# A PSUM bank of its own for one product of the last block, and the same steps in a new order

## The chip, the cores and the metric

The kernel runs on one core of one Trainium2 chip. The metric is the device time of one execution in microseconds, as the median of several runs; lower is better. The core's engines are named as in the profile: PE (TensorE, matmuls), PEld (its weight loads), DVE (VectorE), ACT (ScalarE), POOL (GpSimd) and SP (SyncE, which issues nearly all transfers). PSUM, into which TensorE writes, has eight banks here, each a tile `ps` of 128 × 512 float32.

## The reference

An attention with a decaying state is followed by a two-layer network with a leaky ReLU. B, H, S, D are 4, 8, 768 and 48; the network has 3072 tokens, 384 columns and 2048 hidden columns.

```python
for t in range(S):
    cur = np.einsum('bhd,bhe->bhde', u[None] * kt, vt)
    y[:, :, t] = np.einsum('bhd,bhde->bhe', rt, state + cur)
    state = wt[:, :, :, None] * state + np.einsum('bhd,bhe->bhde', kt, vt)
...
x = y.transpose(0, 2, 1, 3).reshape(B * S, H * D)
h = x @ w_in
out = np.maximum(0.01 * h, h) @ w_out
```

Inputs and outputs are float32; the kernel multiplies in bfloat16 and accumulates in float32.

## The kernel before, in words

**Attention.** The tokens are cut into 24 chunks of 128. Each chunk's four inputs w, k, r and v are loaded by SP (line 841; the first two chunks of each batch are loaded together, line 626) into one of ten `in` buffers. ACT takes logarithms of w (L851); TensorE sums them along the chunk with a triangular matrix (L857) and makes the chunk's total decay (L860); DVE subtracts a chunk's own part (L869); ACT takes exponentials (L878, L883, L887); DVE multiplies r and k by them (`rk`, L541). `rk` is then transposed to `rkT`: for some chunks by TensorE (L552) with a copy out of PSUM on DVE or ACT (L557, L559), for 13 others by a transposing DMA on SP's queue (L904). TensorE makes the scores from `rkT` (L998), DVE masks them (`m`, L928), and TensorE makes the output from the old state (L964) and from the scores (L969). POOL computes the bonus of the current token (L571, L575, L583) and casts v (L591); DVE adds the bonus into `y` (L614). The state goes on by L938, L953 and POOL's L915. `y` is transposed into `xT`, by TensorE (L600, copied by L605 or L607) or by a transposing DMA (L983, 8 chunks).

**Network.** The tokens go through it in 15 blocks of one or two chunks. For each block, up-projections (L1160) fill PSUM banks (`hp`, or `hq` in the last three blocks), and ACT applies the leaky ReLU into `g` (L1175). Down-projections (L1190) accumulate 16 hidden slices into a bank `op`; DVE or ACT copies it out (L1201, L1203) and SP stores it (L1207). The weights are loaded by SP (L462, L467) and cast to bfloat16 by POOL, DVE or ACT (L484, L486, L488).

**The last three blocks** use seven half-size products in place of eight (function `seven`). DVE forms differences of weight quarters once (`mix`, L1044) and, for each block, sums of parts of `g` (L1075, into an `in` buffer and into `g` itself). TensorE runs the products (L1092). They land in the halves of three banks:

```python
b1, b2, b3 = Buf("ps", "op"), Buf("ps", "op2"), Buf("ps", "op2")
px, py, pv, pw, pz = (lambda b=b, x=x: b.t[:, x * HN : (x + 1) * HN]
                      for b, x in ((b1, 0), (b1, 1), (b2, 0), (b2, 1), (b3, 0)))
...
s_c22 = plus(ob, hi(ob), lo(eb), pv, [s_e3, s_7], [eb, b2])
s_3 = products(14.5, b2, [(pw, lambda: sv(2), lambda: qs[:, 1, 1])], [*s_sum["s4"], s_7], stop=True)
s_c12 = plus(oa, hi(oa), lo(eb), pw, [s_e3, s_3], [eb, b2])
```

`take` copies a half bank to SBUF (L1106 on DVE, L1108 on ACT), `plus` adds a half bank to such a copy on DVE (L1113). The four results are c11 and c12 (the two halves of the first chunk's rows, in `oa`) and c21 and c22 (the second chunk's, in `ob`). In the last block c11 and c12 are stored as two halves of 96 KB, and `ob` as one piece of 192 KB (L1143). The products have names: s_1 (px, py), s_7 and then s_3 in one bank (pv and pw), s_6 and s_5 (px, accumulated), s_4 (pz).

**The order of the work.** Each piece above is recorded as a step with its engines and lengths, the steps that it waits for, the buffers that it reads or takes, and a priority. A planner (`Plan.order`) then plays the kernel through with these lengths: an engine that comes free takes the ready step of lowest priority number whose buffers are free. What comes out is one fixed order for all engines, and the buffer that each step gets. The table `RANK` adds a number of its own to the priority of every step, and `FORCE` binds some steps to one of the engines that could run them. On the chip each engine, and SP's queue, works off its instructions in that fixed order, and each waits by semaphores for what it needs. Where the plan leaves TensorE idle in the first 24 us, filler matmuls on zeros are put in (L1232).

Of the kernel before, what the change touches and what calls it, by code (L numbers as in the profile page):

```python
# [23 lines left out]
class Plan:  # L24
# [138 lines left out]
RANK = {0: -59.43, 1: -52.42, 2: -98.27, 3: -101.28, 4: -69.43, 5: 951.62, 6: -68.29, 7: -162.82, 8: -162.92,  # L163
# [144 lines left out]
def kernel(  # L308
# [41 lines left out]
    blocks = [2, 1, 1, 1, 1, 2, 2, 2, 2, 2, 1, 1, 2, 2, 2]  # L350
# [53 lines left out]
    with tc.manual_schedule():  # L404
# [644 lines left out]
        def seven(nb, chs, g, g_done):  # L1049
# [4 lines left out]
            qs = quarters(w_out_b)  # L1054
# [4 lines left out]
            def sv(x):  # L1059
                return sm.t[:].bitcast(BF16).rearrange("p (x i n) -> p x i n", x=3, n=L)[:, x]  # L1060

            groups = [range(0, 4), range(4, 8)] if nb == len(blocks) - 1 else [range(0, 8)]
            s_sum = {}
# [36 lines left out]
            lo = lambda b: lambda: b.t[:, 0:HN]  # L1100
# [166 lines left out]
```

## Time and profile before

| | |
|---|---|
| time, median of 3 runs | 181.15 us |
| the three runs | 181.15, 180.34, 185.15 us |
| profiled execution: time | 180.35 us |
| profiled execution: span of its trace | 178.6 us |
| mean granted TensorE clock | 0.997 |
| busy: PE, DVE, ACT, POOL | 171.6, 130.2, 116.1, 104.7 us |
| transfers | 34.43 MB in 116716 packets, of which 109137 under 512 B |

The span runs from the first to the last instruction of the profiled execution, and the time includes what lies around it. A row of the chain or the timeline gives the start in the span, the length, the engine and the line; "x8" is the number of instructions in one row, and a bracket tells how long the engine was idle ahead of it and what ended that. A row of waits has the engine, who waited for whom, the total in us, the number of times and the longest.

### The profile page before, as it was taken

What the parts mean: (1) busy time and instruction counts of PE and PEld (TensorE: products, weight loads), DVE (VectorE), ACT (ScalarE), POOL (GpSimd) and SP (SyncE); (2) the same over time, 40 slices, a digit from 0 to 9 for tenths busy, and PEclk for the clock granted to TensorE, in tenths of its full rate; (3) what the DMA queues carried; (4) which work ended last, traced back from release to release, by engine and by line L of the source; (5) the groups of instructions that cost most, each with busy time, mean ns of one, the idle gap of its engine ahead of it and who ended that gap; (6) DMA issues with size and microseconds to landing.
All of it is one profiled execution on the core that took longest, in us unless ns stands there. A gap on an engine that the chain in (4) does not pass through costs nothing.

```text
span 178.6 us, 5383 instructions
## 1 busy us (share of the span) xinstructions
PE 171.6 (96%) x2110; PEld 135.0 (76%) x2110; DVE 130.2 (73%) x265; ACT 116.1 (65%) x259; POOL 104.7 (59%) x139
## 2 busy tenths in 40 slices
PE   7898999999999999999999999999999999999992
PEld 2556888866878787787688777777688788799991
DVE  7498953368877989769776379699778778786462
ACT  5668967675887679666467974287385587822830
POOL 5989633665985686947619849339773557400000
PEclk9999999999999999999999999999999999999998
DMA  5999999999999998999999999999999985913004
GB/s 138 261 283 313 372 375 368 186 198 173 205 168 225 190 212 143 193 231 150 170 161 195 196 224 242 137 194 207 145 193 173 245 166 129 232 25 114 2 22 156
DMA packets 116716, 34.43 MB, mean 193 GB/s; under 512 B 109137, under 2 KB 115922, under 8 KB 116690
## 3 DMA queue, kind: packets, MB, share of 16 engines
q1 hardware_dynamic: 116688, 34.09, 96.7%
q8 instruction: 16, 0.26, 0.7%
q14 instruction: 10, 0.08, 0.2%
q10 hardware_dynamic: 2, 0.00, 0.0%
HBM read 25.17 MB, written 4.72 MB: 167 GB/s over the span
## 4 chain that ended last, share of the span: by engine, by line
PE 58%; DMA 14%; SPq 11%; DVE 4%; POOL 4%; ACT 4%; issue 3%; POOLq 0%; DVEq 0%
PE ps L1160 23%; PE ps L1190 14%; SPq L841 10%; PE ps L1092 8%; DMA in<-in_k_dram 5%; DMA xT<-y 3%; DMA in<-in_v_dram 3%; DMA rkT<-rk 2%; POOL ru L571 2%; PE ps L998 2%; DMA in<-in_r_dram 2%; PE ps L552 1%; PE ps L969 1%; PE ps L1232 1%; PE ps L964 1%
## 5 line engine op out<-in xcount | busy, mean ns | idle before, releaser
L1160 PE MATMUL ps<-xT,w_in_b 128*128 128x256 bf16 (+1 forms) x720 | 72.2, 251 | 0.4 <-DMA xT<-y 0.3
L1175 ACT ACTIVATE g<-ps 128x512 bf16<-128x512 f32 x96 | 55.9, 595 | 24.5 <-PE ps L1160 21.3
L1160 PEld LDWEIGHTS <-w_in_b 128*128 128x128 bf16 x720 | 57.6, 98 | 8.5 <-issue 0.5
L1190 PE MATMUL ps<-w_out_b,g 128*128 128x384 bf16 x288 | 55.8, 326 | 0.0
L1190 PEld LDWEIGHTS <-g 128*128 128x128 bf16 x288 | 25.9, 98 | 12.4
L541 DVE TENSOR_TENSOR rk<-in,ps 128x384 bf16<-128x384 f32 x48 | 24.8, 549 | 9.6 <-ACT ps L887 2.2
L571 POOL TENSOR_TENSOR ru<-in,ub 128x384 f32<-128x384 f32 x24 | 23.9, 998 | 13.0 <-DMA in<-in_k_dram 10.6
L928 DVE TENSOR_TENSOR m<-ps,maskb 128x512 bf16<-128x512 f32 x40 | 25.3, 682 | 2.8 <-PE ps L998 2.6
L575 POOL TENSOR_TENSOR ru<-ru,in 128x384 f32<-128x384 f32 x24 | 24.5, 1026 | 3.0 <-DMA in<-in_r_dram 2.5
L915 POOL TENSOR_TENSOR sb<-s,a 128x384 bf16<-128x384 f32 x18 | 15.2, 844 | 11.6 <-ACT a L878 11.5
L583 POOL TENSOR_TENSOR vs<-in,dg 128x384 f32<-128x384 f32 x20 | 17.6, 883 | 4.6 <-DVE dg L579 1.7
L591 POOL CAST vb<-in 128x384 bf16<-128x384 f32 x24 | 12.0, 503 | 9.5 <-DMA in<-in_v_dram 8.3
L869 DVE TENSOR_TENSOR ci<-ps,lw 128x384 f32<-128x384 f32 x20 | 11.1, 555 | 8.3 <-PE ps L860 5.1
L579 DVE TENSOR_REDUCE dg<-ru 128x8 f32<-128x384 f32 x24 | 13.0, 547 | 2.0 <-POOL ru L575 2.0
L851 ACT ACTIVATE lw<-in 128x384 bf16<-128x384 f32 x20 | 10.4, 522 | 5.8 <-DMA in<-in_w_dram 5.7
L614 DVE TENSOR_TENSOR y<-ps,vs 128x384 bf16<-128x384 f32 x20 | 11.0, 553 | 3.9 <-PE ps L969 1.9
L878 ACT ACTIVATE a<-ps 64x4 f32<-64x4 f32 x36 | 6.1, 168 | 8.1 <-DVE ci L869 5.7
L1203 ACT COPY o<-ps 128x384 f32<-128x384 f32 x14 | 6.7, 478 | 5.8 <-PE ps L1190 5.8
L1232 PE MATMUL ps<-zeros 128*128 128x128 bf16 (+1 forms) x41 | 9.1, 337 | 1.3 <-DVE zeros L405 1.3
L887 ACT ACTIVATE ps<-ci 128x384 f32<-128x384 f32 x20 | 9.7, 485 | 0.7 <-DVE ci L869 0.7
L883 ACT ACTIVATE ps<-ps 128x384 f32<-128x384 f32 x20 | 9.4, 469 | 0.8 <-DVE ci L869 0.6
L953 DVE TENSOR_TENSOR s<-ps,sb 128x384 f32<-128x384 f32 x14 | 7.7, 552 | 1.7 <-PE ps L938 1.5
(103 smaller groups left out, 220.9 us busy)
## 6 DMA issues: line engine op xcount, KB each, us to landing
out_dram<-o SPq DMA_DIRECT2D x23, 192.0 KB, 3.1
in<-in_w_dram SPq DMA_DIRECT2D x20, 192.0 KB, 4.3
in<-in_k_dram SPq DMA_DIRECT2D x20, 192.0 KB, 4.7
in<-in_r_dram SPq DMA_DIRECT2D x20, 192.0 KB, 4.3
in<-in_v_dram SPq DMA_DIRECT2D x20, 192.0 KB, 4.2
in<-in_moe_w_out_dram SPq DMA_DIRECT2D x4, 768.0 KB, 10.6
in<-in_moe_w_in_dram SPq DMA_DIRECT2D x4, 384.0 KB, 7.1
in<-in_moe_w_in_dram SPq DMA_DIRECT2D x2, 768.0 KB, 8.9
```

The costliest lines, as they stand in the source:

```text
L541: (nc.gpsimd if e == "POOL" else nc.vector).tensor_tensor(out=o, in0=x, in1=i, op=ALU.mult)
L571: lambda e: nc.gpsimd.tensor_tensor(out=ru.t[:], in0=kv(), in1=ubv, op=ALU.mult),
L575: lambda e: nc.gpsimd.tensor_tensor(out=ru.t[:], in0=ru.t[:], in1=rv(), op=ALU.mult),
L579: lambda e: nc.vector.tensor_reduce(out=dg.t[:], in_=ru.t[:], axis=AX.X, op=ALU.add),
L583: lambda e: nc.gpsimd.tensor_tensor(out=vs.t[:], in0=vv(), in1=dg.t[:].unsqueeze(2).to_broadcast([128, H, D]), op=ALU.mult),
L841: nc.sync.dma_start(out=part(i)(), in_=src[b, :, t0 : t0 + L, :].rearrange("h p d -> p h d"))
L915: lambda e: nc.gpsimd.tensor_tensor(out=sb.t[:].rearrange("p g a d -> p (g a) d"), in0=s_in.t[:].rearrange("p g a d -> p (g a) d"), in1=a_ ...
L928: lambda e, par=par: nc.vector.tensor_tensor(out=m.t[:, par, :, :], in0=sc[par].t[:].rearrange("p (g t) -> p g t", g=NP), in1=maskb[:].uns ...
L1092: nc.tensor.matmul(o(), lhsT=x()[:, i, :], rhs=y()[:, i, :], start=fresh, stop=(stop and i == ii[-1]), skip_group_check=True)
L1160: nc.tensor.matmul(hp.t[:, a * N : (a + 1) * N], lhsT=w_in_b[:, t, (j + a) * 128 : (j + a + 1) * 128], rhs=xT[:, t, c0 : c0 + N], start=(a ...
L1175: lambda e, hp=hp, g=g, j=j, J=J, N=N: nc.scalar.activation(out=g.t[:, j : j + J, 0:N], in_=hp.t[:, 0 : J * N].rearrange("p (a n) -> p a n ...
L1190: nc.tensor.matmul(op.t[:, 0:DM], lhsT=g.t[:, j, off : off + 128], rhs=w_out_b[:, j, :], start=(j == 0), stop=(j == NJ - 1))
```

## The change

The edit to the code is in `seven`, for the last block alone: pw gets a bank `b4` of its own (`own`), so the product s_3 starts a bank (`start=own`) and no longer waits for s_7, which wrote pv. Besides, `RANK` has new numbers for 1082 of its 1088 steps, and `FORCE` binds other steps to engines (63 entries against 69). Both tables come from a search for an order, this time with smaller lengthenings of the steps while it searched. The steps themselves and their recorded lengths stay as they were. Lines behind the tables move down by 2 to 6: L1092 of before is L1096 of after, L1113 is L1117, L1143 is L1149, L1160 is L1166, L841 is L843, L904 is L906.

```diff
-RANK = {0: -59.43, 1: -52.42, 2: -98.27, 3: -101.28, 4: -69.43, 5: 951.62, 6: -68.29, 7: -162.82, 8: -162.92,
...
+RANK = {0: -32.93, 1: -33.92, 2: -148.03, 3: -147.74, 4: -75.54, 5: -50.53, 6: -92.91, 7: -193.52, 8: -193.62,
...
-FORCE = {4: "ACT", 24: "DVE", 27: "ACT", 30: "DVE", 33: "ACT", 47: "ACT", 57: "ACT", 59: "ACT", 60: "ACT", 62:
...
+FORCE = {4: "ACT", 6: "DVE", 24: "DVE", 27: "ACT", 33: "DVE", 47: "ACT", 62: "ACT", 80: "ACT", 83: "ACT", 86:
...
             b1, b2, b3 = Buf("ps", "op"), Buf("ps", "op2"), Buf("ps", "op2")
+            own = nb == len(blocks) - 1
+            b4 = Buf("ps", "op3") if own else b2
             px, py, pv, pw, pz = (lambda b=b, x=x: b.t[:, x * HN : (x + 1) * HN]
-                                  for b, x in ((b1, 0), (b1, 1), (b2, 0), (b2, 1), (b3, 0)))
+                                  for b, x in ((b1, 0), (b1, 1), (b2, 0), (b4, 1 - own), (b3, 0)))
...
-            s_3 = products(14.5, b2, [(pw, lambda: sv(2), lambda: qs[:, 1, 1])], [*s_sum["s4"], s_7], stop=True)
-            s_c12 = plus(oa, hi(oa), lo(eb), pw, [s_e3, s_3], [eb, b2])
+            s_3 = products(
+                14.5, b4, [(pw, lambda: sv(2), lambda: qs[:, 1, 1])], [*s_sum["s4"], None if own else s_7], start=own,
+                stop=True)
+            s_c12 = plus(oa, hi(oa), lo(eb), pw, [s_e3, s_3], [eb, b4])
```

More of the change, by code (lines that the diff above doesn't have):

```diff
@@ L162 @@
 TY = (0.95, 24, 0.7, -0.6)
-RANK = {0: -59.43, 1: -52.42, 2: -98.27, 3: -101.28, 4: -69.43, 5: 951.62, 6: -68.29, 7: -162.82, 8: -162.92,
[133 rows of a table removed]
-FORCE = {4: "ACT", 24: "DVE", 27: "ACT", 30: "DVE", 33: "ACT", 47: "ACT", 57: "ACT", 59: "ACT", 60: "ACT", 62:
-    "ACT", 80: "ACT", 83: "DVE", 86: "DVE", 89: "ACT", 103: "DVE", 113: "DVE", 115: "DVE", 116: "ACT", 120:
-    "ACT", 122: "POOL", 124: "POOL", 126: "ACT", 128: "ACT", 129: "POOL", 131: "POOL", 132: "ACT", 134: "DVE",
-    135: "POOL", 137: "DVE", 138: "DVE", 141: "POOL", 143: "DVE", 158: "DVE", 160: "ACT", 187: "ACT", 189:
-    "DVE", 198: "ACT", 202: "DVE", 240: "ACT", 262: "DVE", 278: "ACT", 280: "ACT", 309: "DVE", 311: "ACT",
-    325: "DVE", 384: "DVE", 422: "ACT", 436: "DVE", 493: "DVE", 613: "ACT", 737: "ACT", 771: "ACT", 785:
-    "ACT", 799: "ACT", 849: "ACT", 855: "ACT", 877: "DVE", 883: "ACT", 905: "ACT", 933: "ACT", 939: "DVE",
-    953: "ACT", 967: "ACT", 1003: "ACT", 1031: "DVE", 1034: "ACT", 1039: "ACT", 1076: "ACT", 1081: "ACT"}
+RANK = {0: -32.93, 1: -33.92, 2: -148.03, 3: -147.74, 4: -75.54, 5: -50.53, 6: -92.91, 7: -193.52, 8: -193.62,
[135 rows of a table added]
+FORCE = {4: "ACT", 6: "DVE", 24: "DVE", 27: "ACT", 33: "DVE", 47: "ACT", 62: "ACT", 80: "ACT", 83: "ACT", 86:
+    "DVE", 116: "DVE", 118: "DVE", 124: "DVE", 126: "ACT", 128: "ACT", 129: "DVE", 131: "ACT", 137: "DVE",
+    141: "DVE", 143: "POOL", 144: "ACT", 158: "DVE", 160: "DVE", 173: "ACT", 189: "DVE", 198: "DVE", 238:
+    "DVE", 240: "DVE", 254: "DVE", 311: "ACT", 325: "DVE", 341: "ACT", 343: "DVE", 422: "DVE", 436: "ACT",
+    444: "DVE", 493: "DVE", 501: "DVE", 605: "DVE", 613: "ACT", 737: "ACT", 771: "DVE", 785: "ACT", 799:
+    "ACT", 821: "ACT", 827: "DVE", 849: "ACT", 855: "DVE", 877: "ACT", 883: "ACT", 905: "ACT", 911: "DVE",
+    933: "DVE", 939: "ACT", 953: "ACT", 967: "ACT", 995: "DVE", 998: "DVE", 1003: "ACT", 1031: "DVE", 1034:
+    "ACT", 1039: "ACT", 1076: "ACT"}
 @with_exitstack
```

268 rows, old and new, of the table RANK are left out of this document.

## The prediction

> **What bounds the kernel now.** I read the page's busy shares and the slices first.
>
> ```profile
> span 178.6 us, 5383 instructions
> PE 171.6 (96%) x2110; PEld 135.0 (76%) x2110; DVE 130.2 (73%) x265; ACT 116.1 (65%) x259; POOL 104.7 (59%) x139
> DMA  5999999999999998999999999999999985913004
> q1 hardware_dynamic: 116688, 34.09, 96.7%
> PE 58%; DMA 14%; SPq 11%; DVE 4%; POOL 4%; ACT 4%; issue 3%; POOLq 0%; DVEq 0%
> ```
>
> Two things are full at once. TensorE is busy for 171.6 of 178.6 us, and the transfer engines are busy in nearly every slice (4.5 us each) up to 143 us. The chain of waits shares the span out accordingly: TensorE 58%, transfers and SP's queue 25%. DVE, ACT and POOL have 48, 63 and 74 us of idle time. The table by stage shows when each limit holds:
>
> ```profile
> core 0: us, PE busy (x) PEld busy (x) DVE busy (x) ACT busy (x) POOL busy (x), PEclk, DMA share, GB/s
> 0.00:19.00 19.00, 16.17 (x224) 10.00 (x225) 15.08 (x43) 12.79 (x28) 15.23 (x31) 1.00 1.05 256
> 19.00:64.00 45.00, 44.84 (x601) 35.47 (x601) 30.72 (x59) 33.41 (x72) 29.50 (x37) 1.00 1.04 241
> 128.00:152.00 24.00, 24.00 (x326) 20.02 (x324) 18.51 (x35) 17.33 (x41) 13.87 (x18) 1.00 0.95 184
> 157.00:168.00 11.00, 11.00 (x129) 10.43 (x125) 7.90 (x19) 4.51 (x9) 0.00 (x0) 1.00 0.20 57
> 168.00:176.00 8.00, 7.39 (x86) 6.95 (x83) 4.80 (x14) 2.68 (x7) 0.00 (x0) 1.00 0.19 66
> ```
>
> The transfer share (rows overlap, so it can pass 1) is 0.95 or more in the stages shown up to 152 us and 0.2 after 157 us, where TensorE alone sets the pace. What links the two stages is in the chain in order of time:
>
> ```profile
> 19.05 1.47 PE ps L1160 x12
> ...
> 144.38 0.17 PE ps L964 x4
> ...
> 152.55 3.59 DMA rkT<-rk
> 156.18 0.40 PE ps L998 x8
> 157.05 1.32 PE ps L1092 x16
> 158.55 0.20 PE ps L969 x8
> 163.37 5.24 PE ps L1160 x48
> 168.60 5.32 PE ps L1092 x64
> 174.41 0.37 DVE o L1113
> 174.82 0.83 PE ps L1092 x8
> 175.68 0.36 DVE o L1113
> ```
>
> The up-projections begin at 19.05. The last transposing DMA that carries rkT lands, the last scores (L998) run at 156.18, the last attention products (L969) at 158.55, and from there TensorE has only up-projection matmuls (L1160) and the products of the last blocks (L1092). These stand 5.24/48 = 0.109 and 5.32/64 = 0.083 us apart. The program has 54 of the first kind and 128 of the second behind that last L969 group: 158.75 + 54 × 0.109 + 128 × 0.083 = 175.26. The last group in fact ends at 175.65. So one stall of 0.4 us is in this stage, and the rows at 174.41 and 174.82 show it.
>
> **The change, first part: the bank.** The stall, in the timeline of the end:
>
> ```profile
> 164.06 5.18 ACT L1175 ACTIVATE g<-ps 128x512 bf16<-128x512 f32 x8 [3.64 <-PE ps L1160]
> ...
> 173.42 1.15 PE L1092 MATMUL ps<-in,g 128*128 128x192 bf16 x12
> 174.32 0.10 PEld L1092 LDWEIGHTS <-in 128*128 128x128 bf16 x1
> 174.82 0.82 PE L1092 MATMUL ps<-w_out_b,in 128*128 128x192 bf16 x8 [0.25 <-DVE o L1113]
> 175.68 0.36 DVE L1113 TENSOR_TENSOR o<-ps,o 128x192 f32<-128x192 f32 x1 [0.65 <-PE ps L1092]
> ```
>
> The last product (s_3, into pw) goes into the right half of the bank whose left half (pv) DVE is still adding from. The twelve matmuls before it would let it start at 173.42 + 12 × 0.083 = 174.42; its weights are in at 174.32, but it starts at 174.82, when DVE's add is done. With pw in a bank of its own the order of the changed program has no wait on any of those eight matmuls, so 0.40 us goes. The new bank was an up-projection bank; its reader, ACT's L1175, is through by 169.24, five us earlier, so nothing new is waited for. The last two products also change places: s_3 now runs before s_4, so the last matmul group is s_4, and three adds of 0.36 us follow: c12 can start 0.66 us (8 × 0.083) before the last group ends, c22 is next, c21 waits for that end. DVE then has 0.66 us for two adds of 0.36 us, so c21 is at most 0.1 us late. TensorE ends at 175.65 − 0.40 = 175.25, the last add at about 175.65 instead of 176.04.
>
> The price is in the store behind it. Now the last store is the whole 192 KB row block (c21 and c22) and not the half (c12):
>
> ```profile
> out_dram<-o SPq DMA_DIRECT2D x3, 192.0 KB, 2.0
> out_dram<-o SPq DMA_DIRECT2D x2, 96.0 KB, 1.6
> ```
>
> These are the stores of the end alone. 2.0 − 1.6 = 0.4 us goes back. The bank is worth −0.40 + 0.05 + 0.40 = +0.05 us: nothing. Bounds: −0.4 (the larger store is hidden after all) and +0.4 (c21 late by a whole add).
>
> **The change, second part: the order.** The comparison of the two programs, engine by engine, shows what the new ranks and forced engines do.
>
> SP: the same 144 transfers, of which the first 14 stand in the same order. The last rkT transpose is the 134th in both, and the 133 ahead of it are the same in kind and number (80 loads of single chunks, 17 stores, 12 rkT and 6 xT transposes, 8 paired loads, 10 weight loads). While the transfer engines stay full, its landing is set by that volume and not by its order. Behind it stand the same ten transfers. Cost 0; the stream's fill is the cover, and rival 1 is what happens without it.
>
> PE: the same 2069 working matmuls; the fillers (L1232) go from 15 wide and 26 narrow ones to 17 and 22.
>
> ```profile
> L1232 PE MATMUL ps<-zeros 128*128 128x512 bf16 x15 | 5.8, 514 | 1.3 <-DVE zeros L405 1.3
> L1232 PE MATMUL ps<-zeros 128*128 128x128 bf16 x26 | 4.2, 235 | 0.0
> ```
>
> 2 × 0.51 − 4 × 0.24 = +0.1 us, in a stage where TensorE waits for the first chunks. Behind the last L969 group stand the same 54 and 128 matmuls. Between the last scores and the end stand 66 up matmuls and 136 products instead of 54 and 144, with one attention group fewer: 12 × 0.109 − 8 × 0.083 = +0.64, less 0.37 (eight L969 and four L964 matmuls, 0.20 and 0.17 us): +0.3 us if the last rkT lands at the same moment. Before has waits of its own in this stretch (158.37, the end of sixteen L1092 from 157.05, to 158.55), 0.2 us. I take +0.1, bounds −0.2 and +0.3.
>
> POOL, DVE and ACT: four weight casts leave POOL (7 to 3), two for DVE, two for ACT; copies out of PSUM move both ways. In all DVE has 7 instructions more, ACT 3 and POOL 4 fewer.
>
> ```profile
> L484 POOL CAST w_out_b<-in x3: 827/1214/1215, 27.0 to 33.4; 128x768 bf16<-128x768 f32 x3
> L486 DVE CAST w_out_b<-in x5: 549/559/1200, 25.6 to 33.4; 128x768 bf16<-128x768 f32 x5
> 27.04 1.20 DVE L486 CAST w_out_b<-in 128x768 bf16<-128x768 f32 x1 [0.46 <-DMA in<-in_moe_w_out_dram]
> 31.14 1.22 POOL L484 CAST w_out_b<-in 128x768 bf16<-128x768 f32 x1 [1.27 <-DMA in<-in_moe_w_out_dram]
> ```
>
> DVE gets about 7 × 0.55 = 3.9 us on 130.2, POOL loses 4 × 0.83 = 3.3 us. All of it lies beside TensorE, which is full from 19 to 64 us (44.84 of 45.00). If that cover is gone in one place, the cost is one copy, 0.36 to 0.56 us. I take 0, bounds −0.5 and +0.5.
>
> One rule speaks against moving casts to DVE: the Trainium skill, "SBUF — State Buffer", section "SBUF: two separate sides", says that DVE and GpSimd share a port pair as an exclusive lock, and that whichever starts first holds it for its whole instruction. The trace agrees: at 27.04 the DVE cast, started just after POOL's, took 1.20 instead of 0.56 us, and at 31.14 POOL's, started after DVE's, took 1.22 instead of 0.83. By it two more DVE casts would cost POOL up to 2 × 0.39 = 0.8 us, against the 3.3 us that POOL is relieved of; the sum would stay where it is.
>
> **The sum.** +0.05 (bank) + 0.1 (fillers) + 0.1 (last stretch) + 0 (the rest) = +0.25 us, and its bounds together are −1.0 and +1.3. The profiled execution took 180.35 us for its span of 178.6, so it comes out at 180.6, between 179.4 and 181.7. The three runs before were 180.34, 181.15 and 185.15, so that execution is at their low end and 0.8 under their median. The new median should scatter like them; I put 0.2 on it: 180.8 us.
>
> **Rivals.** 1, slower: the transfer stream runs dry behind a waiting SP. SP issues in order, so a transpose whose source is late holds every load behind it.
>
> ```profile
> SPq L904 <- PE ps L1160: 5.9, 5, 2.1
> SPq L904 <- DVE rk L541: 2.9, 1, 2.9
> in<-in_w_dram SPq DMA_DIRECT2D x20, 192.0 KB, 4.3
> ```
>
> Of the waits that have loads behind them the longest is now 2.9 us, and a load lands 4.3 us after its issue, so what is in flight covers them. It decides where waits in a row exceed 4.3 us. The new order puts two xT and one rkT transpose in a row (107th to 109th). Were each to wait 2.9 us, 8.7 − 4.3 = 4.4 us would be lost in a full stream and never come back: 184.8 us, 2.4% slower. Against it: those three would all have to be as late as the latest one now. Two such waits would cost 1.5 us, 181.9. (The Trainium skill, "DMA: Bandwidth & Descriptors", section "Anatomy of one DMA — SWDGE (gpsimd) path", says that semaphore waits happen on the issuing sequencer before dispatch; this is that rule at work, and SP's waits above agree.)
>
> 2, faster: the new order removes TensorE's other waits. Idle is 178.6 − 171.6 = 7.0 us, of which 2.95 lie after the last matmul (175.65) and 1.3 before the first:
>
> ```profile
> PE ps L1232 <- DVE zeros L405: 1.3, 1, 1.3
> PE ps L1160 <- DMA xT<-y: 0.3, 1, 0.3
> ```
>
> 2.75 us are left in many small pieces. All of them gone would give 177.6, 1.5% faster; over 2% would need an earlier start as well, and the first 14 transfers are unchanged.
>
> 3, the bank does nothing: another wait takes its place, such as the products that wait for ACT's copy of px. Then the larger store alone counts, +0.4 on 180.35 and the other terms' 0.2: 181.0. It lies inside the forecast's bounds and is counted apart for its cause.
>
> **How the numbers follow.** Forecast (179.4 to 181.7) 0.63; rival 1 0.14, half of it over 2%; rival 2 0.13, a third of it over 2% by way of the start; rival 3 0.10. Two per cent, 3.6 us, is about what a measurement of this kernel tells from no change. So faster 0.05; slower 0.07 and 0.02 for scatter like the run of 185.15, 0.09; same 0.86. The range takes half of rival 2 and the two-wait form of rival 1 with the runs' own scatter: 179.0 to 183.0.
>
> **What would show it.** Right: the last L1092 group has no idle time before it, TensorE's last group ends about 19 us after the last rkT landing, the last store is 192 KB with about 2.0 us to landing, and the transfers stay full to 143 us. Wrong: a slice of the transfers below 8 before that, SP waits over 4.3 us, the last scores later than 157 us, or a first up-projection more than 1 us away from 19.05.

## The result, and the profile after

The changed kernel takes 181.15 us (median of 20 runs), before 181.53 us (20 runs, the three listed above among them), and the ratio is 1.0057, 95% interval 1.003 to 1.0084. The ratio compares fast runs alone, and ten of before's runs (181.92 to 186.97 us) lie more than 1.5% above its fastest, which is why it is over 1 although before's median is the higher one. So the changed kernel is slower by about 1.0 us. Two later measurements on two chips, beside before each time, gave 1.0077 (1.0052 to 1.0102) and 1.0091 (1.0064 to 1.0117), that is 1.4 and 1.6 us. I had forecast no change.

The page of the profiled execution, 0.9 us longer than that of before:

```profile
span 179.5 us, 5373 instructions
PE 171.4 (96%) x2104; PEld 134.4 (75%) x2108; DVE 132.9 (74%) x272; ACT 115.4 (64%) x256; POOL 100.3 (56%) x135
DMA  5999999998999999999899999999999996813004
PE 66%; DMA 12%; DVE 6%; POOL 5%; ACT 4%; SPq 3%; issue 2%; DVEq 0%; ACTq 0%; POOLq 0%
```

TensorE has the same work within 0.2 us, and the transfers are as full as before. What changed is the chain: TensorE's share rose from 58 to 66%, SP's queue fell from 11 to 3%. The table by stage, with the columns and the stages of the one before:

```profile
0.00:19.00 19.00, 16.20 (x209) 9.57 (x213) 15.32 (x43) 12.89 (x28) 15.23 (x31) 1.00 1.05 257
19.00:64.00 45.00, 43.84 (x595) 34.07 (x595) 32.60 (x65) 31.64 (x68) 25.02 (x33) 1.00 1.16 237
128.00:152.00 24.00, 23.46 (x321) 19.60 (x321) 18.26 (x35) 16.47 (x39) 16.18 (x21) 1.00 1.00 190
168.00:176.00 8.00, 7.93 (x93) 7.59 (x90) 5.39 (x16) 3.29 (x8) 0.00 (x0) 1.00 0.15 53
```

From 19 to 64 us TensorE is busy for 43.84 us where it was 44.84, from 128 to 152 us for 23.46 where it was 24.00; from 64 to 128 us it waits 0.39 us less. So TensorE now waits in two stages in which it had hardly waited. The first of these two rows of waits (who waited for whom, total, times, longest) has no counterpart in before; for the second, before had 0.4 us:

```profile
PE ps L859 <- ACT lw L853: 0.8, 2, 0.4
PE ps L554 <- DVE rk L543: 0.6, 2, 0.5
```

L859 is the cumulative sum of a chunk ("cum"), L853 the logarithm of its w on ACT. The chain (first row) and the timeline show one of the two waits with what lay ahead of it; the length of a transfer is its whole way from issue to landing:

```profile
46.58 5.94 DMA in<-in_w_dram
52.54 0.52 ACT L853 ACTIVATE lw<-in 128x384 bf16<-128x384 f32 x1 [0.88 <-DMA in<-in_w_dram]
53.11 0.32 PE L859 MATMUL ps<-lw,trev 128*128 128x384 bf16 x1 [0.32 <-ACT lw L853]
```

A w load took 5.94 us, ACT stood for it, and TensorE, in order, stood behind ACT. In before the cum of that chunk ran at 53.55, more than a microsecond after its logarithm (51.87 to 52.39); now it follows 0.05 us behind. The same rows of before, for the chunk two places ahead and for this one:

```profile
42.80 0.52 ACT L851 ACTIVATE lw<-in 128x384 bf16<-128x384 f32 x1 [1.77 <-DMA in<-in_w_dram]
43.37 0.32 PE L857 MATMUL ps<-lw,trev 128*128 128x384 bf16 x1
51.87 0.52 ACT L851 ACTIVATE lw<-in 128x384 bf16<-128x384 f32 x1
53.55 0.33 PE L857 MATMUL ps<-lw,trev 128*128 128x384 bf16 x1
```

The first pair is a warning: before, too, had a late w load (ACT waited 1.77 us) and a cum 0.05 us behind its logarithm, and TensorE did not wait there, since it had other work up to that moment. A short distance alone is not yet a loss.

The end of the program, and the stores of the end with their median time to landing:

```profile
173.13 0.49 PE L1096 MATMUL ps<-in,g 128*128 128x192 bf16 x4
173.69 0.82 PE L1096 MATMUL ps<-in,in 128*128 128x192 bf16 x8
174.67 0.82 PE L1096 MATMUL ps<-w_out_b,in 128*128 128x192 bf16 x8
175.33 0.82 PE L1096 MATMUL ps<-in,g 128*128 128x192 bf16 x8
175.60 0.95 DVE L1117 TENSOR_TENSOR o<-ps,o 128x192 f32<-128x192 f32 x3 [0.37 <-PE ps L1096]
...
out_dram<-o SPq DMA_DIRECT2D x3, 192.0 KB, 1.9
out_dram<-o SPq DMA_DIRECT2D x2, 96.0 KB, 1.6
```

The product s_3 at 174.67 (`w_out_b,in`) has no idle time ahead of it: the 0.40 us stall of before is gone. The last group now ends at 176.15, 0.5 us later than before's 175.65. From the last add's end to the end of the span there are 179.5 − 176.55 = 2.95 us; before had 178.6 − 176.04 = 2.56. I put that down to the larger store: 0.39 us (e3 below takes 0.29 of it back).

### The profile page after: what moved, and what is told of

Read it like the earlier page. It is cut to its first block, busy times and chain, and to the rows that moved or that the text cites. A ratio compares the mean times of both kernels' runs of the same rounds, so it can differ in the third digit from the quotient of the medians.

```text
span 179.5 us, 5373 instructions
## 1 busy us (share of the span) xinstructions
PE 171.4 (96%) x2104; PEld 134.4 (75%) x2108; DVE 132.9 (74%) x272; ACT 115.4 (64%) x256; POOL 100.3 (56%) x135
## 4 chain that ended last, share of the span: by engine, by line
PE 66%; DMA 12%; DVE 6%; POOL 5%; ACT 4%; SPq 3%; issue 2%; DVEq 0%; ACTq 0%; POOLq 0%
PE ps L1166 26%; PE ps L1196 16%; PE ps L1096 6%; DMA in<-in_v_dram 3%; DMA in<-in_w_dram 3%; SPq L843 3%; DMA in<-in_k_dram 3%; PE ps L1000 3%; DMA in<-in_r_dram 2%; POOL ru L573 2%; PE ps L971 2%; POOL ru L577 2%; PE ps L966 2%; PE ps L554 1%; PE ps L859 1%
## 5 line engine op out<-in xcount | busy, mean ns | idle before, releaser
L1166 PE MATMUL ps<-xT,w_in_b 128*128 128x256 bf16 (+1 forms) x720 | 73.1, 251 | 0.5 <-DMA xT<-y 0.5
L1166 PEld LDWEIGHTS <-w_in_b 128*128 128x128 bf16 x720 | 57.8, 98 | 9.2 <-DMA xT<-y 0.8
L1196 PE MATMUL ps<-w_out_b,g 128*128 128x384 bf16 x288 | 56.8, 326 | 0.0
L573 POOL TENSOR_TENSOR ru<-in,ub 128x384 f32<-128x384 f32 x24 | 24.6, 1029 | 17.2 <-DMA in<-in_k_dram 15.4
L1196 PEld LDWEIGHTS <-g 128*128 128x128 bf16 x288 | 25.4, 97 | 11.7
L585 POOL TENSOR_TENSOR vs<-in,dg 128x384 f32<-128x384 f32 x20 | 16.5, 828 | 5.9 <-DVE dg L581 3.7
L853 ACT ACTIVATE lw<-in 128x384 bf16<-128x384 f32 x20 | 10.5, 523 | 4.6 <-DMA in<-in_w_dram 4.5
L1238 PE MATMUL ps<-zeros 128*128 128x128 bf16 (+1 forms) x35 | 7.8, 347 | 1.7 <-DVE zeros L407 1.3
L554 PE MATMUL ps<-ident,rk 128*128 128x128 bf16 x88 | 8.1, 220 | 0.7 <-DVE rk L543 0.6
L1209 ACT COPY o<-ps 128x384 f32<-128x384 f32 x12 | 5.7, 478 | 4.2 <-PE ps L1196 4.0
```

Source lines behind the costliest of these rows:

```text
L573: lambda e: nc.gpsimd.tensor_tensor(out=ru.t[:], in0=kv(), in1=ubv, op=ALU.mult),
L585: lambda e: nc.gpsimd.tensor_tensor(out=vs.t[:], in0=vv(), in1=dg.t[:].unsqueeze(2).to_broadcast([128, H, D]), op=ALU.mult),
L1166: nc.tensor.matmul(hp.t[:, a * N : (a + 1) * N], lhsT=w_in_b[:, t, (j + a) * 128 : (j + a + 1) * 128], rhs=xT[:, t, c0 : c0 + N], start=(a ...
L1196: nc.tensor.matmul(op.t[:, 0:DM], lhsT=g.t[:, j, off : off + 128], rhs=w_out_b[:, j, :], start=(j == 0), stop=(j == NJ - 1))
```

## The experiments

Runs e1 to e4 shared a chip and the runs of before, and so did e5 to e8, e9 to e11, e12 to e14 and e15 to e18. "Old order" is that of before, "new order" that of after. In e12 to e16 one or two loads bring one head of eight, so these kernels leave out seven heads of one or two inputs and compute something else; they serve for times and waits alone. Most edits move single steps in the finished order:

```diff
         order = plan.order(pools)
+        for i, j in ((209, 754), (269, 787)):       # step i right behind step j
+            order.remove(i)
+            order.insert(order.index(j) + 1, i)
```

The table has TensorE's busy time in two stretches of 16 us, as the table by stage of each run gives it, and the ratio to before. The first row is before's own profile. The gaps that some expectations name (1.4 to 1.9 us between 40 and 56 us in the new order, 0.7 to 0.9 in the old) were counted in another way, which no view here shows; I go by the table.

| run | order and edit | PE 40–56 | PE 128–144 | ratio (95%) |
|---|---|---|---|---|
| before | old | 15.94 | 16.00 | 1 |
| after | new | 15.24 | 15.46 | 1.0057 (1.003–1.0084) |
| e1 | old, bank | 15.93 | 16.00 | 0.9985 (0.9959–1.0012) |
| e2 | new, two cums later | 15.37 | 15.31 | 1.0087 (1.0065–1.011) |
| e3 | new, small store last | 15.80 | 15.31 | 1.0079 (1.0051–1.0108) |
| e4 | new, two w loads sooner | 15.32 | 15.31 | 1.0105 (1.0054–1.0157) |
| e5 | new | 15.56 | 15.31 | 1.0077 (1.0052–1.0102) |
| e6 | new, dg behind ci | 15.38 | 15.91 | 1.0053 (1.0034–1.0072) |
| e7 | new, mix elsewhere | 15.23 | 15.91 | 1.0051 (1.003–1.0071) |
| e8 | old, bank, store behind rkT | 15.96 | 16.00 | 0.9964 (0.9943–0.9986) |
| e9 | new, two chains later | 15.73 | 15.31 | 1.0085 (1.0058–1.0111) |
| e10 | new, e9 + e6 + e3 | 15.84 | 15.92 | 1.0036 (1.0016–1.0057) |
| e11 | old, store behind rkT, no bank | 16.00 | 16.00 | 0.9983 (0.9962–1.0005) |
| e12 | new, one load cut | 15.56 | 15.30 | 1.0034 (1.0006–1.0062) |
| e13 | e8, one load cut | 15.85 | 16.00 | 0.9934 (0.9908–0.996) |
| e14 | new, e6 + e3, one load cut | 15.70 | 15.91 | 0.999 (0.9962–1.0018) |
| e15 | new, two loads cut | 16.00 | 15.31 | 1.0035 (1.0012–1.0058) |
| e16 | e8, two loads cut | 16.00 | 16.00 | 0.9916 (0.9894–0.9939) |
| e17 | new | 15.20 | 15.31 | 1.0091 (1.0064–1.0117) |
| e18 | e8 again | 16.00 | 16.00 | 0.9974 (0.9956–0.9992) |

**The bank alone (e1).** The old order stays; `b4` is a free bank (`b4.t = pools["ps"][1]`) and s_3 starts it.

> The order of before, every instruction in its old place on every engine; alone the last product of the last block (s_3) writes a bank of its own. Theory (the bank takes away one stall, the loss comes from the new order): the 0.40 us that the last L1092 group of before waited at 174.42 is gone, the 96 KB store stays last, so the kernel ends 0.3 to 0.4 us sooner than before: ratio 0.998. Rival (the bank itself costs, by one more bank held at the end): slower than before, 1.002 or more. Rival (the stall was slack, the store or DVE sets the end): 1.000, and the wait turns up at DVE's last sums instead.

0.9985 is the direction of the theory, not told apart from no change by the time alone. Its trace has no wait at the last group, but TensorE stands at the last scores for the last rkT:

```profile
155.54 0.40 PE L998 MATMUL ps<-rkT 48*128 48x128 bf16 x8 [0.91 <-DMA rkT<-rk]
```

So the bank is not what costs; the new order is. And the old order has a wait that after does not have (after's last scores ran at 156.63 without one).

**Later cums, and sooner loads (e2, e4).** e2 is the diff above. e4 puts the two w loads one place forward in the order: `order.insert(order.index(j), i)` for (203, 176) and (263, 206).

> After, with two TensorE steps in other places: the cumulative sums (L859 and the four L862) that waited for a w load at 41.14 and 52.47 stand one down group and one sums-and-up pair later, so that TensorE has 0.65 and 0.84 us more work ahead of them. Nothing else is moved. Theory (TensorE, in order, stood behind a cum placed close behind its load): about 1.0 us less than after, so 0.999 to 1.001 of before, and the 0.8 us at L859 are gone. Rival (the late transfers set the time, TensorE waits at another place by as much): no change from after, 1.005 to 1.006 of before. Rival (the start stage is what was lost): no change from after either, with the gaps of 6 to 24 us as they were.

> After, with two of the 35 first SP issues swapped with the one ahead of them: the w loads that ended the waits at 41.3 and 52.5 us are issued one load (about 1.1 us) sooner, ahead of an r and of a v load. TensorE's order is that of after. Theory (a cum behind a late load): both loads land about 1 us sooner, the waits at L859 shrink from 0.8 us to 0 to 0.2, and the time falls by 0.7 to 1.0 us against after: 1.000 to 1.002 of before. Rival (the stream as a whole is late): another load is late in its place, as after, 1.005.

Both won nothing (1.0087 and 1.0105; 15.37 and 15.32 us busy), and both theories missed. My theory of single cums standing too close falls; a wait stands at the next link. First e2, then two rows of e4:

```profile
43.88 0.40 PE L554 MATMUL ps<-ident,rk 128*128 128x128 bf16 x4 [0.51 <-DVE rk L543]
```

```profile
40.07 0.55 DVE L543 TENSOR_TENSOR rk<-in,ps 128x384 bf16<-128x384 f32 x1 [1.27 <-DMA in<-in_r_dram]
40.68 0.40 PE L554 MATMUL ps<-ident,rk 128*128 128x128 bf16 x4 [0.75 <-DVE rk L543]
```

In e2 the later cum makes ci late on DVE, and the rk product of the chunk ahead stands behind ci. In e4 the w load came sooner at the price of an r load, and the transposes stood for that.

**The store (e3).** Steps (1083, 1078), (1084, 1079), (1087, 1085): s_3, its add and its store last.

> After, with its last three sums in the sequence of before: s_4 ahead of s_3 on TensorE, c12 last on DVE, and the 96 KB store of c12 last on SP; the bank stays. Theory (the end is a sum: last TensorE group, one DVE sum, one store): 0.3 to 0.4 us less than after, 1.003 to 1.004 of before, with TensorE's last group as late as in after. Rival (the size of the last store does not matter, since both stores end together): as after, 1.0057. The waits at L859 should be there as in after, which shows whether they come back in another execution: 0.8 us in 2 times by the theory, elsewhere or gone if they were one execution's jitter.

In the trace the theory holds for the store:

```profile
175.58 0.36 DVE L1117 TENSOR_TENSOR o<-ps,o 128x192 f32<-128x192 f32 x1 [0.24 <-PE ps L1096]
```

The last add ends at 175.94 and the span at 178.6, so 2.66 us lie behind it where after has 2.95. In time it does not show: 1.0079 (I had 1.003 to 1.004), against after's 1.0077 and 1.0091 on other chips. A difference of 0.3 us is below what these comparisons can tell.

**After again (e5), and the stage at 130 us (e6, e7).** In every profile of e2 to e5 TensorE lacks 0.7 us between 128 and 144. e6 moves step 594 behind 641, e7 moves step 988 behind 621.

> The changed kernel itself once more, unaltered, beside before and the next three on one chip, as the foot for their differences and as a second look at its waits. Theory: the same places stall in every execution of the new order: TensorE loses 0.5 to 1.1 us between 40 and 56 us, and 0.7 to 0.9 us ahead of the cum at about 131.5 to 133; it is 1.005 to 1.010 of before. Rival (the waits of the first trace were that execution's jitter): the stalls are elsewhere or less than half as long, ratio under 1.004.

> After, with one swap on DVE: the reduce dg (L581) that waits until POOL's ru (L577) ends at about 129.8 us stands behind the sum ci (L871) instead of ahead of it. In the last three kernels of the new order this chain ran: DVE waits 0.94 us for ru, ci starts 1.2 us after its cum, ACT's three exponentials 1.2 us later, the next w's logarithm stands behind them on ACT, and TensorE stands 0.85 us at the cum L859 for it. Theory (that chain is a loss of the new order): ci starts about 1 us sooner, the 0.85 us at L859 near 132 go, and the kernel ends 0.5 to 0.85 us sooner than after, 0.3 to 0.5% of before, unless the last rkT, which then sets the last scores, gives part of it back. Rival (TensorE waits for the last rkT instead by as much): as after, with the wait at L1000 near 155.

> After, with the one DVE mix (L1046, 128x1536) of 125.6 us moved behind the ci of about 133 us; its first reader comes at 148. In the new order this mix and its neighbour ran while POOL multiplied: POOL's ru took 1.71 and 1.60 us there against 1.00 elsewhere, and the mix 1.14 to 1.28 against 0.95. Theory (POOL and DVE slow each other, and that lengthening is what pushes ru, dg, ci and the next cum): POOL's ru at 126.2 falls to about 1.0 us, dg no longer waits 0.9 us, the 0.85 us at L859 near 132 shrink to 0.2 or less, and the kernel is as e6 (0.5 to 0.85 us below after). Rival (only the place of dg on DVE matters, not the lengthening): ru stays at 1.6 or the wait stays, as after.

Here is the chain in e5, engine by engine from the timeline:

```profile
126.30 1.28 DVE L1046 TENSOR_TENSOR in<-w_out_b,in 128x1536 bf16<-128x1536 bf16 x1
126.85 1.60 POOL L577 TENSOR_TENSOR ru<-ru,in 128x384 f32<-128x384 f32 x1
129.49 1.00 POOL L577 TENSOR_TENSOR ru<-ru,in 128x384 f32<-128x384 f32 x1
130.52 0.55 DVE L581 TENSOR_REDUCE dg<-ru 128x8 f32<-128x384 f32 x1 [0.94 <-POOL ru L577]
130.99 0.55 DVE L871 TENSOR_TENSOR ci<-ps,lw 128x384 f32<-128x384 f32 x1
131.57 0.17 ACT L880 ACTIVATE a<-ps 64x4 f32<-64x4 f32 x1 [1.23 <-DVE ci L871]
132.67 0.52 ACT L853 ACTIVATE lw<-in 128x384 bf16<-128x384 f32 x1
133.25 0.32 PE L859 MATMUL ps<-lw,trev 128*128 128x384 bf16 x1 [0.69 <-ACT lw L853]
```

POOL's ru, begun while DVE's mix ran, takes 1.60 us instead of 1.00. DVE's dg, first in line, waits 0.94 us for the next ru; ci stands behind dg although its cum (129.49) is long done; ACT's exponentials wait 1.23 us for ci; the next logarithm stands behind them; and TensorE stands behind that, four engines from where the delay began. No load is late in it. In e6 and then in e7:

```profile
129.80 0.56 DVE L871 TENSOR_TENSOR ci<-ps,lw 128x384 f32<-128x384 f32 x1 [0.79 <-ACT a L880]
132.07 0.32 PE L859 MATMUL ps<-lw,trev 128*128 128x384 bf16 x1
```

```profile
126.71 1.00 POOL L577 TENSOR_TENSOR ru<-ru,in 128x384 f32<-128x384 f32 x1
129.77 0.55 DVE L581 TENSOR_REDUCE dg<-ru 128x8 f32<-128x384 f32 x1 [0.33 <-POOL ru L577]
132.50 0.32 PE L859 MATMUL ps<-lw,trev 128*128 128x384 bf16 x1
```

Either edit takes the wait at L859 away, and TensorE is busy for 15.91 us of the 16. The medians fall from e5's 180.97 to 180.41 and 180.57, 0.56 and 0.40 us (six to nine runs each, on one chip). Two more pairs on one chip each differ by e6's edit together with e3's store: e9 to e10 (180.87 to 180.05) and e12 to e14 (180.35 to 179.92), and TensorE's busy time from 128 to 144 rises from 15.31 to 15.92 and from 15.30 to 15.91. Two different ways to break one chain win about the same amount, so this part of the loss is shown, from POOL's lengthening down to TensorE. e1, in the old order, has such a lengthening too (POOL's bonus at 126.51), but no reduction that waits for POOL stands ahead of ci: ci waits for nothing but its cum, and the next cum does not wait:

```profile
126.51 1.48 POOL L583 TENSOR_TENSOR vs<-in,dg 128x384 f32<-128x384 f32 x1 [0.61 <-DVE dg L579]
128.35 0.56 DVE L869 TENSOR_TENSOR ci<-ps,lw 128x384 f32<-128x384 f32 x1 [0.42 <-PE ps L860]
130.83 0.32 PE L857 MATMUL ps<-lw,trev 128*128 128x384 bf16 x1
```

**The old order's last wait (e8, e11).** Step 934, an output store, goes behind 679, the last rkT transpose, in e8 with the bank, in e11 without.

> Before's order with the bank (as e1), and one more swap on SP: the output store issued just ahead of the last rkT transpose goes behind it. In e1 TensorE stood 1.07 us at the last scores for that rkT, whose rk was ready 1.9 us before its issue. Theory (in the old order the last transfer on SP sets the last scores): the transpose is issued and lands 0.7 to 0.8 us sooner, TensorE's wait at L998 near 154 falls to 0.3, and the kernel is 0.5 to 0.7 us below e1: 0.994 to 0.996 of before. Rival (other transfers in flight hold the transpose, not its issue): it lands when it did, 0.998 as e1.

> Before, with the one swap on SP that e8 has (the store ahead of the last rkT goes behind it) and without the bank. Theory (bank and swap are two gains that add, 0.15 to 0.2% each): 0.998 to 0.9985, TensorE not waiting for the last rkT, and the 0.40 us at the last L1092 group back; the difference from e8's 0.9964 is the bank. Rival (the bank is worth nothing in time): 0.9965 as e8.

e8 is 0.9964, e18 (the same kernel on another chip) 0.9974, both intervals below 1: this version beats both kernels. The last scores no longer wait; the next row is e8's, and the second is e11's last s_3, which waits again as in before (due at 171.50 + 12 × 0.083 = 172.50):

```profile
154.37 0.40 PE L998 MATMUL ps<-rkT 48*128 48x128 bf16 x8
```

```profile
171.50 1.15 PE L1092 MATMUL ps<-in,g 128*128 128x192 bf16 x12
172.91 0.82 PE L1092 MATMUL ps<-w_out_b,in 128*128 128x192 bf16 x8 [0.25 <-DVE o L1113]
```

From e11 (0.9983) to e8, on two chips, the bank brings 0.19%, from before to e1 0.15%: about 0.3 us twice, each alone within its uncertainty, and both agree with the 0.4 us that the traces show.

**The stage at 40 to 56 us (e9, e10, e12 to e16).** e9 adds to e2 the moves (210, 185), ci behind an rk product, and (188, 770), transposes behind a down group. e10 is e9, e6 and e3 together. The cut of e12 to e14 (206) and of e15 and e16 (176 and 206):

```diff
+                    few = 1 if lds[i] in (176, 206) else H
                     nc.sync.dma_start(
-                        out=part(i)(), in_=src[b, :, t0 : t0 + L, :].rearrange("h p d -> p h d"))
+                        out=part(i)()[:, 0:few, :], in_=src[b, 0:few, t0 : t0 + L, :].rearrange("h p d -> p h d"))
```

> After, with the chain of two chunks moved as a whole between 40 and 54 us: the cums of 40.6 and 51.6 as in e2 (one down group, and one sums-and-up pair, later), and with them what e2 left in the way: on DVE the rk product whose k load has landed goes ahead of the ci of the next chunk, and its transposes on TensorE stand one down group later. Theory (in this stretch the new order stands each link of the chain load, logarithm, cum, ci, exponential, rk, transposes closer behind the one before than the loads land; moving one link, as e2 and e4 did, only moves the wait to the next): TensorE's idle gaps of 40 to 56 us fall from 1.4 to 1.9 us to 0.9 or less, and the time by 0.4 to 0.8 us against after: 1.003 to 1.005 of before. Rival (the stream of loads itself holds this stretch back, whatever stands behind it): the gaps move on to the next chunk, 55 to 66 us, and the time stays, 1.007.

> After with all three mended together: the two chains of e9, dg behind ci of e6, and the 96 KB store last of e3. Theory (the loss of the new order is the sum of these three, and the bank's 0.4 us stays won): after's 1.0077 less 0.003 for e9, 0.0025 for e6 and 0.002 for the store: 1.000, within 0.002. Rival (TensorE, once sooner, waits for the last rkT as it did in the old order): 1.003, with a wait of 0.4 us or more at L1000 near 155.

> After, with one of its transfers cut to an eighth: the v load just ahead of the w load that lands near 52 us brings one head of eight (24 KB in place of 192), so seven heads of v of one chunk are not loaded and the output differs there. Theory (the stream of loads holds TensorE back between 40 and 56 us in the new order, which is why moving single links there won nothing in e2, e4 and e9): the w load lands about 1 us sooner, TensorE's gaps of 40 to 56 us fall from 1.7 to about 1.0, and the time by 0.4 to 0.7 us against after: 1.004 to 1.005 of before. Rival (the gaps come from how the engines' steps stand to one another, not from the loads): gaps and time as in after, 1.007 to 1.009.

> The control: e8 (the old order with the bank and the store behind the last rkT) with the same v load of the same chunk cut to one head of eight. Theory (in the old order TensorE has about 0.7 us more work in hand there, so the loads are not what it waits for): the gaps of 40 to 56 us stay at 0.8 and the time within 0.2 us of e8: 0.995 to 0.9965. Rival (one transfer less simply shortens the program by what it takes, about 1 us, in either order): 0.991.

> After with the two mended places that won time (dg behind ci of e6, and the 96 KB store last of e3, which e10 had too) and the same load cut as in e12. Theory (the loss of the new order against before is these places and the loads of 40 to 56 us): 1.0077 less 0.0025, less 0.002, less 0.003: 0.999 to 1.001. Rival (something else of 0.5 us or more is still lost in the new order): 1.003 or more.

> After, with two transfers cut to an eighth: the r load just ahead of the w load that lands near 41 us, and the v load of e12 (one head of eight is brought in each, so the output differs for the other heads). On one chip with after, e8 and the control. Theory (between 40 and 56 us the new order waits for the stream of loads): both waits of TensorE there shrink, its gaps of 40 to 56 us fall from 1.7 us to 0.9 or less, and the time is 0.5 to 0.8 us below after on the same chip. Rival (one or two transfers less save no TensorE time, what e12 won was the difference between chips): gaps stay over 1.3 us and the time is within 0.2 us of after.

> The control: e8 with the same two loads of the same chunks cut. Theory: TensorE's gaps of 40 to 56 us stay at 0.7 to 0.9 and the time within 0.2 us of e8 on the same chip. Rival (less traffic helps either order alike): 0.5 to 0.8 us below e8.

> After unaltered, as the foot of e15 on this chip. Both theories: 1.006 to 1.009 of before; TensorE's gaps of 40 to 56 us 1.4 to 1.9, of 128 to 144 us 1.3.

> e8 unaltered, as the foot of e16 on this chip, and the second measurement of the one version that beat both kernels: 0.995 to 0.9975 of before, gaps of 40 to 56 us 0.7 to 0.9. If e8's gain was that chip's, 0.998 or more.

Six kernels of the new order have no edit that touches this stage (after, e3, e5, e6, e7, e17), and TensorE is busy there for 15.20 to 15.80 us: so much does one kernel's execution differ from another's. e9 missed: its 15.73 us lie within that spread, the time is after's (1.0085), and no gap moved on to 56 to 72 us either (15.98 of 16 us busy). e10 recovered about half of the loss (1.0036), not all; its trace has no wait for the last rkT, so the rival fails as well. Then two loads were cut. The tables by stage of e17, e15, e18 and e16, all on one chip, in this order (busy TensorE, clock, transfer share, GB/s):

```profile
40.00:56.00 16.00, 15.20 (x210) 1.00 1.24 169
128.00:144.00 16.00, 15.31 (x223) 1.00 1.07 197
```

```profile
40.00:56.00 16.00, 16.00 (x227) 1.00 1.08 170
128.00:144.00 16.00, 15.31 (x228) 1.00 1.13 199
```

```profile
40.00:56.00 16.00, 16.00 (x217) 1.00 1.04 199
```

```profile
40.00:56.00 16.00, 16.00 (x222) 1.00 1.09 200
```

With two loads cut the new order's 0.80 us of waiting between 40 and 56 are gone, which is outside the spread, and the untouched loss at 128 to 144 is still there. So in the traces this wait is one for loads. In the old order there is no such wait in these two profiles (0.15 us at most in the others). The times do not confirm that this is what divides the two orders: cutting the loads took e15 from 181.11 to 179.76 us, and the control e16 from 178.92 to 177.88, 0.56% and 0.58% of before. The theory had at most 0.2 us for the control; its rival is nearer. The two profiles of the old order differ by 0.2 us in span only (176.5 and 176.3), since e18's profiled run was one of its fastest (178.19, with runs up to 179.37). Where the control's microsecond comes from in the other runs stays open. e12 (1.0034) and e13 (0.9934, where I had 0.995 to 0.9965) had shown the same on another chip, and for that reason e14's 0.999 can't be read as a closed sum.

What is left: about 0.4 to 0.6 us of the loss is shown to be the chain at 130 us; at 40 to 56 us TensorE waits in every profile of the new order with all its loads (0.2 to 0.8 us idle), but the part of that in the time is not settled. Between 19 and 40 us TensorE is busy for 20.0 to 20.6 us of 21 in the new order and 20.6 to 21.0 in the old; no run separates that.

## Why the prediction was wrong, point by point

**The bank, −0.40 + 0.05 + 0.40.** Right in each term, by the traces. The stall is gone; the last add ends 0.40 us after the last group (176.15 to 176.55) as it did before (175.65 to 176.04), where I allowed 0.05 more; the larger store costs 0.39, of which e3 takes 0.29 back. Rival 3 (another wait takes its place) came half true: a wait of 173.69 − (173.13 + 4 × 0.083) = 0.23 us stands ahead of the twelve products before s_3. The profile names nothing that it waits for.

**Fillers and start, +0.1.** The first up-projections begin at 18.95, in before at 19.05, so nothing was lost there that could be seen.

**The last stretch, +0.1 (−0.2 to +0.3).** Too small. From the last scores to the last group's end it is 156.63 to 176.15, 19.52 us; before 19.47, with 0.40 of stall. So the rest of it grew by 0.45. The added work that I had worked out as +0.3 and the new wait of 0.23 us are about that. The stretch hardly varies: 19.52 or 19.53 us in the profiles of the new order with all loads, 19.04 or 19.05 in e1, e8 and e18. I had taken off 0.2 for a wait of before from 158.37 to 158.55. That was misread from the chain; TensorE has work there:

```profile
158.21 0.33 PE L964 MATMUL ps<-sb,rkT 128*128 128x96 bf16 x4
```

**SP 0, and POOL, DVE and ACT 0 (±0.5).** This is the step that failed. I counted instructions and transfers, found the same numbers, and named TensorE's fullness from 19 to 64 us as the cover ("All of it lies beside TensorE, which is full"). But that fullness is not a property of the work; it belongs to the order before. Under the new order TensorE waits 1.0 us more from 19 to 64 us and 0.54 more from 128 to 152. Over the whole of 19 to 152 us (133 us) it is busy for 132.29 us in before, 132.56 in e1 and 132.85 in e18, and for 131.13, 131.00 and 130.11 in after, e5 and e17. How the new order makes it wait is shown for the chain at 130 us: a sum stands on DVE behind a reduction that waits for POOL. For 19 to 64 us it is not shown; that the links stand closer together there is my reading of one cum, and moving cums back (e2) won nothing. The bound of one copy (0.5 us) was also too small: I had a delay paid once, beside TensorE, and at 130 us it is handed on through DVE and ACT, each in order, to TensorE.

**The rule on the shared port.** I applied it to the casts alone and priced it by POOL's own time (0.8 us, off the path). In e5 it is a mix that meets POOL: 1.60 us for POOL's 1.00, 1.28 for the mix that takes 0.95 elsewhere. e7 shows that the price is set by who stands behind POOL: 0.40 us of the program for 0.60 us of POOL. The Trainium skill, "SBUF — State Buffer", section "SBUF: two separate sides", has a DVE operation with two SBUF inputs and a GpSimd operation that reads SBUF exclude each other. e5 agrees to within 0.15 us: had POOL's 1.00 us begun when the mix ended, at 127.58, ru would have ended at 128.58; it ended at 128.45.

**The rivals.** 1, the stream running dry behind SP, did not happen: SP's share of the chain fell to 3%, and after the first slice, the same in both, no slice before 143 us is below 8. 2, TensorE's other waits vanish, went the other way. What I listed as signs of a wrong forecast (a slice below 8, SP waits with loads behind them, a late start, last scores after 157) stayed quiet, since none of them looks at TensorE's own waits by stage.

**The size.** Of the +0.9 us of the span, 0.5 are TensorE's later end and 0.39 the larger store. TensorE's end is net of the bank's 0.40: the order cost about 0.9 us, where I had 0.2. That is a low figure, since before's profiled execution (180.35 us) was not one of its quick ones; beside the experiments before's medians are 179.42 to 179.75. By the three ratios after loses 1.0, 1.4 and 1.6 us, and as the bank's gain and the store's cost are equal, so much did the order cost. The chain at 130 us is 0.4 to 0.6 of it, the wait in the last stretch 0.23 by the trace, and the cause of the rest stays open.

## What to carry to other kernels

A new order with equal counts on every queue is not free, because an engine that is full under one order can wait under another. Follow each step that TensorE needs back through the engines ahead of it, and look at what each of them stands behind; the distance to the step that feeds it does not tell enough. Price a lengthening by who stands behind it in order, not by the idle time of the engine that suffers it. And when one stall has been removed, look for the next transfer that the following stage waits for: here one store moved behind the last transpose was worth about as much as the bank (0.2% each by the ratios, neither clear of its uncertainty alone, both together clear).

## What the runs showed of the hardware that I had not expected

Moving a mix of DVE, 128 × 1536 in bfloat16, out of POOL's way shortened a POOL multiplication from 1.60 to 1.00 us. A 192 KB load, of a kind that took 4.7 us to landing in the median of that execution, took 5.94. And before's runs scatter: its medians beside the experiments, on four chips, lie close together (179.42 to 179.75 us), but its first twenty runs have 181.53 and reach from 179.0 to 186.97. Against effects of half a microsecond, differences are safe only between kernels run together.
